# A one-core attention and FFN kernel: eight pooled PSUM banks, the token gate on VectorE, memory in column tiles, and a newly tuned instruction plan

## The chip, the cores and the metric

The kernel runs on one core of a Trainium2 chip. The metric is device microseconds of one execution. Most executions of one kernel agree within 0.3%. All runs told here are at a granted TensorE clock of 0.99 to 1.00. PE is TensorE (its matrix engine), DVE is VectorE, ACT is ScalarE, POOL is GpSimd, SP is the engine that issues most DMAs. PSUM is the memory that the matmuls of this kernel write, used as eight banks of 128x512 fp32; SBUF is the on-chip memory of its other tiles.

## The reference

Two branches read the same `x` (2048 tokens, 512 features) and are mixed by a gate per token. In short:

```python
g = sigmoid((x * gate_w).sum(-1, keepdims=True))        # one number per token
a = A(x)      # 32 heads of 16, 4 segments of 512 tokens, causal softmax inside a segment,
              # plus a linear memory carried from segment to segment:
#   a_mem = phi(q) @ M / (phi(q) @ z + 1e-6);   o = gh * a_mem + (1 - gh) * a_dot
#   M += phi(k).T @ v;  z += phi(k).sum()       # after each segment; then o @ wo
b = (relu(x @ W_gate) * (x @ W_up)) @ W_down            # 1792 wide
return g * a + (1 - g) * b
```

The kernel factors `1 - g` out, so that what the attention branch needs per token is the ratio `g / (1 - g)`.

## The kernel before

Nothing is scheduled by hand line by line. The program describes its work as tasks: an engine, an assumed duration, a priority (`key`, lower first), dependencies and a PSUM bank. A small list scheduler, the plan, runs over these tasks at build time with its assumed durations. The order in which it starts them becomes the order of instructions on each engine. On the chip each engine takes its instructions in that order: in the changed kernel's trace all 2214 matmuls fall on the plan's tasks one by one, in the order emitted. If an instruction is not ready, everything behind it on that engine waits (the chain near 57 us, below, shows it).

The parts that the change touches, with cuts marked:

```python
def run(self):                                   # the plan
    ...
    for t in sorted((t for t in ready if t.avail <= now), key=rank):
        if busy.get(t.eng, 0.0) > now: continue
        ...                                      # takes a PSUM bank if one is free
        if mode.get(t.eng) != t.mode:            # PE: full array, row tiles or column tiles
            t.dur += SWITCH + (126 if t.mode and mode.get(t.eng) else 0)
...
sp = psum.tile([P, 4, L], F32, name="sp")        # four banks: scores only
wb = [psum.tile([P, L], F32, name=f"wb{b}") for b in range(4)]   # four banks: all else
...
# assumed durations in ns, by engine
plan.add("DVE", 690, ...)   # a 128x512 eviction from PSUM
plan.add("DVE", 460, ...)   # KTe, KTo: masked copies of K transposed, SBUF to SBUF
plan.add("DVE", 830, ...)   # phi: two SBUF operations
plan.add("ACT", 1880, ...)  # exponential of 128x2048 scores
plan.add("POOL", 640 * len(diags), ...)          # causal mask of the exponentials, affine_select

def gate_tasks(seg):
    def pe():                                    # token gate: 16 matmuls with ONE column each
        for t in range(4):
            for ci in range(NC):
                nc.tensor.matmul(bank(sl)[:, t:t + 1], lhsT=xT[...], rhs=gw[:, ci:ci + 1], ...)
    a = plan.add("PE", 420, key, pe, ...)
    ...                                          # exp, then an fp32 matmul spreads the ratios
def memory(seg):                                 # M and z: 16 matmuls, 128 x 136, in two banks
    ...
    a = plan.add("PE", 1000, key, pe, ...)
```

A unit is four pairs of heads of one segment: 16 units in all. Each has five score fills (eight or four row-tiled matmuls into the four score banks), five exponentials on ACT, masks on POOL, and two groups of column-tiled value matmuls. Projections and FFN matmuls of 128x512 fill the rest of PE.

The softmax here doesn't subtract the row's maximum and nothing guards it: scores larger than these inputs give would overflow.

Of the kernel before, what the change touches and what calls it, by code (L numbers as in the profile page):

```python
# [12 lines left out]
P = 128  # L13
# [12 lines left out]
SWITCH = 100.0  # L26
RQ = 5
RE = 8
RH = 16


class Task:




    def __init__(self, eng, dur, key, emit, deps=(), lat=100, need=None, frees=(), after=None,
                 mode=None):
        self.eng, self.dur, self.key, self.emit, self.mode = eng, dur, key, emit, mode
        self.deps = [d for d in deps if d is not None]  # L40
        self.lat, self.need, self.frees, self.after = lat, need, tuple(frees), after
        self.avail = 0.0


class Slot:
    def __init__(self, kind):
        self.kind, self.banks, self.left = kind, (), 0


class Plan:  # L50



    def __init__(self, nbanks):
        self.tasks = []
        self.free = {i: 0.0 for i in range(nbanks)}

    def add(self, *a, **k):
        t = Task(*a, **k)
        self.tasks.append(t)  # L60
        return t

    def pick(self, slot, now):
        ok = [b for b in sorted(self.free) if self.free[b] is not None and self.free[b] <= now]
        if slot.kind == 2:
            for b in ok:
                if b % 2 == 0 and b + 1 in ok:
                    return (b, b + 1)
            return None
        for b in ok:  # L70
            if b ^ 1 not in ok:
                return (b,)
        return (ok[-1],) if ok else None

    def run(self):
        users = {}
        for t in self.tasks:
            t.wait = len(t.deps) + (t.after is not None)
            for d in t.deps:
                users.setdefault(id(d), []).append(t)  # L80
            if t.after is not None:
                users.setdefault(id(t.after), []).append(t)
            for s in t.frees:
                s.left += 1
        ready = [t for t in self.tasks if t.wait == 0]
        busy, mode = {}, {}
        now, order = 0.0, []
        left = len(self.tasks)
        while left:
            progressed = True  # L90
            while progressed:
                progressed = False
                def rank(t):
                    turn = t.mode and mode.get(t.eng) and t.mode != mode[t.eng]
                    return (bool(turn), t.key)
                for t in sorted((t for t in ready if t.avail <= now), key=rank):
                    if busy.get(t.eng, 0.0) > now:
                        continue
                    if t.need is not None and not t.need.banks:
                        got = self.pick(t.need, now)  # L100
                        if got is None:
                            continue
                        t.need.banks = got
                        for b in got:
                            self.free[b] = None
                    if mode.get(t.eng) != t.mode:
                        t.dur += SWITCH + (126 if t.mode and mode.get(t.eng) else 0)
                        mode[t.eng] = t.mode
                    t.start = now
                    busy[t.eng] = now + t.dur  # L110
                    t.done = now + t.dur + t.lat
                    order.append(t)
                    ready.remove(t)
                    left -= 1
                    for s in t.frees:
                        s.left -= 1
                        if s.left == 0:
                            for b in s.banks:
                                self.free[b] = t.done
                    for u in users.get(id(t), ()):  # L120
                        u.wait -= 1
                        u.avail = max(u.avail, t.start + t.dur if u.after is t else t.done)
                        if u.wait == 0:
                            ready.append(u)
                    progressed = True
            if not left:
                break
            times = [t.avail for t in ready if t.avail > now]
            times += [b for b in busy.values() if b > now]
            times += [f for f in self.free.values() if f is not None and f > now]  # L130
            assert times, "the plan is stuck"
            now = min(times)
        self.end = max(t.done for t in order)
        return order
# [3 lines left out]
def kernel(  # L138
# [21 lines left out]
    rpool = ctx.enter_context(tc.tile_pool(name="rpool", bufs=3))  # L160
    psum = ctx.enter_context(tc.tile_pool(name="psum", bufs=1, space=bass.MemoryType.PSUM))

    def sb(shape, dtype, name):
        return wpool.tile(shape, dtype, name=name)


    xT = [sb([P, NC, L], BF16, f"xT{i}") for i in range(3)]
    wq_sb = sb([P, NC, D], BF16, "wq_sb")
# [6 lines left out]
    gw = sb([P, NC], BF16, "gw")  # L175
    betab = sb([P, H], BF16, "betab")

    E = [sb([P, 4, L], BF16, f"E{i}") for i in range(RE)]
    x0 = E[RE - 1]
    clock = [3300.0]  # L180
    plan = Plan(4)

    def arrival(nbytes):
        clock[0] += nbytes / 340.0
        return plan.add("in%d" % len(plan.tasks), 0.0, 0.0, None, lat=clock[0])

    def load(eng, dst, src, nbytes):
        eng.dma_start(out=dst, in_=src)
        return arrival(nbytes)

    def load_cols(eng, t, ap, c0, c1):
        k = ap.shape[0] // P
        return load(eng, t[:, :, c0:c1], ap.rearrange("(c p) n -> p c n", p=P)[:, :, c0:c1],
                    k * P * (c1 - c0) * 2)

    def load_xT(seg):
        nc.sync.dma_start_transpose(out=xT[seg % 3][:], in_=x[seg * L:(seg + 1) * L, :])
        return arrival(L * D * 2 * 1.3)

    FP = [(0, 512), (512, 1024), (1024, 1408), (1408, F)]  # L200
    got_x, got_g, got_u = {}, {}, {}
    def load_halves(dst, src, k, nbytes):
        src = src.rearrange("(c p) n -> p c n", p=P)
        nc.sync.dma_start(out=dst[:, 0:k // 2], in_=src[:, 0:k // 2])  # L204
        nc.scalar.dma_start(out=dst[:, k // 2:k], in_=src[:, k // 2:k])
        return arrival(nbytes)

    got_x0 = load_halves(x0, x[0:L, :], 4, L * D * 2)
    got_q = [load_halves(wq_sb, A_wq, NC, D * D * 2)] * 2
    got_k = [load_cols(nc.sync, wk_sb, A_wk, 0, D)] * 2  # L210
    got_v = load_cols(nc.scalar, wv_sb, A_wv, 0, D)
    nc.scalar.dma_start(out=betab[:], in_=A_beta.partition_broadcast(P))
    with nc.allow_non_contiguous_dma(reason="1 KB"):
        nc.scalar.dma_start(out=gw[:], in_=gate_w.rearrange("(c p) -> p c", p=P))
    got_gw = arrival(0)

    def load_gu(i):
        got_g[i] = load_cols(nc.sync, wg_sb, B_W_gate, *FP[i])
        got_u[i] = load_cols(nc.sync, wu_sb, B_W_up, *FP[i])

    def load_wd(a, b):
        return load(nc.sync, wd_sb[:, a:b, :],
                    B_W_down.rearrange("(c p) n -> p c n", p=P)[:, a:b, :], (b - a) * P * D * 2)

    load_gu(0)
    load_gu(1)
    got_x[1] = [load_xT(1)]
    load_gu(2)
    load_gu(3)
    got_d = [load_wd(0, 7), load_wd(7, NF)]  # L230
    got_o = load_cols(nc.sync, wo_sb, A_wo, 0, D)
    got_x[2] = [load_xT(2)]


    junk = sb([P, L], BF16, "junk")
    nc.vector.memset(junk[:], 0.0)
# [7 lines left out]
    for j in range(4):  # L244
# [7 lines left out]
                            pattern=[[0, NC], [16, 8], [0, HW]], channel_multiplier=-1)  # L252

    fold = sb([P, 4, 32], F32, "fold")
    nc.gpsimd.memset(fold[:], 0.0)
    pbm = sb([P, 4], F32, "pbm")
    nc.vector.memset(pbm[:], 0.0)
    for b in range(4):
        nc.gpsimd.affine_select(out=fold[:], in_=fold[:], compare_op=ALU.not_equal, fill=1.0,
                                base=-32 * b, pattern=[[0, 4], [-1, 32]], channel_multiplier=1)  # L260
        nc.vector.memset(pbm[32 * b:32 * b + 32, b:b + 1], 1.0)
    rblk = sb([P, 4, 4], F32, "rblk")
# [5 lines left out]
    grc = [sb([P, NC, 2, 2, 16], F32, f"grc{i}") for i in range(2)]  # L268

# [11 lines left out]
    got_gates = plan.add("DVE", 900, 0.0, head_gates, [got_eb], 100)  # L281


    sp = psum.tile([P, 4, L], F32, name="sp")
    wb = [psum.tile([P, L], F32, name=f"wb{b}") for b in range(4)]
    QT = [sb([P, L], BF16, f"QT{i}") for i in range(RQ)]
    KTe = [sb([P, L], BF16, f"KTe{i}") for i in range(RQ)]
    KTo = [sb([P, L], BF16, f"KTo{i}") for i in range(RQ)]
    pqT = [sb([P, L], BF16, f"pqT{i}") for i in range(RQ)]
    pK = [sb([P, 4, D], BF16, f"pK{i}") for i in range(2)]  # L290
    Vp = [sb([P, 4, H, 18], BF16, f"Vp{i}") for i in range(2)]
    oT = [sb([P, NC, L], BF16, f"oT{i}") for i in range(2)]
    hT = [sb([P, L], BF16, f"hT{i}") for i in range(RH)]
    T = [sb([P, 2, L], F32, f"T{i}") for i in range(2)]
# [425 lines left out]
```

## Time and profile before

The time was 282.37 us (median of 3 runs, 282.19 to 282.45). The profiled execution has a span of 280.8 us. Two lines of its first page, span and busy time with the share of the span and the number of instructions:

```profile
span 280.8 us, 5327 instructions
...
PE 272.8 (97%) x2122; PEld 113.4 (40%) x2122; DVE 205.7 (73%) x427; ACT 196.6 (70%) x176; POOL 87.6 (31%) x144
```

Then the chain that ended last, followed back from the last instruction, by engine and by line of the kernel:

```profile
## 4 chain that ended last, share of the span: by engine, by line
PE 92%; ACT 3%; DMA 3%; DVE 1%; issue 0%; SPq 0%; ACTq 0%
```

PE is 92% of this chain. So PE sets the time and the others mostly keep up. But a busy PE is not a PE at its peak, so its time was taken apart from the starts of the matmuls in the trace. A 128x512 matmul streams in 216 ns, four row or column tiles together in the same time. Every change between full, row-tiled and column-tiled matmuls costs 93 to 98 ns more (median by kind of change, counted from start to start after subtracting the last group's streaming) and, averaged over whole stretches, about 117 ns. A stall is counted wherever the gap from start to start exceeds the streaming time, and 97 ns at a change, by more than 45 ns. The last row but one is what is left over, since changes are charged at 117 ns and stalls counted from 97. From the first transpose of x to the end of PE:

| part, us | before |
|---|---|
| streaming | 243.9 |
| 193 changes of tiling at 0.117 | 22.6 |
| one-column gate matmuls and fp32 folds, beyond streaming | 2.0 |
| memory matmuls, beyond streaming | 0.2 |
| stalls | 4.0 |
| left over | -1.3 |
| measured, 5.45 to 276.86 us | 271.4 |

Only about 6 us of this (gate, memory, stalls) is neither streaming nor changes of tiling, and of these two the change can save a little. The start is where 1.5 us of the stalls are. In the timeline of PE (start, duration, line, operation; a gap and what ended it in brackets) only half of the 16 Q matmuls run before PE waits for wk:

```profile
6.35 2.19 PE L327 MATMUL wb<-xT,wq_sb 128*128 128x512 bf16 x8
9.55 1.47 PE L327 MATMUL wb<-xT,wk_sb 128*128 128x512 bf16 x6 [1.01 <-DMA wk_sb<-in_A_wk_dram]
```

Three groups of instructions that come up again (count, then busy us and mean ns of one, then idle time before them): the masked K copy on DVE, the memory matmuls and the one-column gate matmuls.

```profile
L435 DVE TENSOR_SCALAR KTe<-kt,mcol_e 128x512 bf16<-128x512 bf16 x16 | 6.9, 436 | 0.1
...
L592 PE MATMUL wb<-Vp,pK 128*128 128x136 bf16 x48 | 3.5, 226 | 0.0
...
L360 PE MATMUL wb<-gw,xT 128*128 128x1 bf16 x64 | 2.2, 163 | 0.0
```

And DVE's busy time in stretches of 10 us (stretch, its length, busy us with the number of instructions, granted clock, DMA share, GB/s):

```profile
20.00:30.00 10.00, 7.89 (x20) 1.00 1.10 342
30.00:40.00 10.00, 8.85 (x20) 1.00 0.65 104
40.00:50.00 10.00, 8.28 (x16) 1.00 0.14 28
50.00:60.00 10.00, 8.10 (x19) 1.00 0.01 2
```

From 10 to 90 us DVE is busy 65.7 of 80 us, well above its 73% over the whole span.

### The profile page before, as it was taken

Reading aid. Unit: us, or ns where it says so; the run is one execution under the profiler, and the core shown is the slowest. Engines: PE = TensorE matmul, PEld = TensorE weight load, DVE = VectorE, ACT = ScalarE, POOL = GpSimd, SP = SyncE. Lnnn points to the kernel's source line nnn. Section 1 sums busy time; section 2 is a strip of 40 time slices with the busy share of each in tenths; the row PEclk is TensorE's granted clock in tenths of the full one; section 3 lists DMA queues with packets and bytes.
Section 4 is the critical chain, followed back from the end, with each engine's and each line's share of the span. In section 5 each row is a group of like instructions: output and inputs, shape, how many; then the busy total and the mean of one; then the engine's idle time right before and its main releaser. Section 6 shows DMA issues by size and latency. Waiting matters only on the chain.

```text
span 280.8 us, 5327 instructions
## 1 busy us (share of the span) xinstructions
PE 272.8 (97%) x2122; PEld 113.4 (40%) x2122; DVE 205.7 (73%) x427; ACT 196.6 (70%) x176; POOL 87.6 (31%) x144
## 2 busy tenths in 40 slices
PE   8899999999989999999999999999999999999994
PEld 3343444433434343343443344344434343444441
DVE  3588797798994768968997599957898966374221
ACT  3299797988886659888876779898897677723000
POOL 7014233334242332433343424443334243300000
PEclk9999999999999999999999999999999999999999
DMA  7999930013001010000001000000000010000011
GB/s 230 316 255 349 208 49 19 4 22 75 19 2 39 21 37 2 19 2 19 0 11 47 21 21 2 0 2 0 2 0 2 19 39 21 0 2 0 0 37 39
DMA packets 24488, 13.71 MB, mean 49 GB/s; under 512 B 13968, under 2 KB 24464, under 8 KB 24464
## 3 DMA queue, kind: packets, MB, share of 16 engines
q1 hardware_dynamic: 22720, 12.32, 16.5%
q10 hardware_dynamic: 1744, 1.06, 1.3%
q8 instruction: 16, 0.26, 0.4%
q14 instruction: 8, 0.07, 0.1%
HBM read 8.14 MB, written 2.10 MB: 36 GB/s over the span
## 4 chain that ended last, share of the span: by engine, by line
PE 92%; ACT 3%; DMA 3%; DVE 1%; issue 0%; SPq 0%; ACTq 0%
PE wb L327 73%; PE sp L478 9%; PE wb L518 7%; DMA wk_sb<-in_A_wk_dram 3%; ACT E L499 2%; PE wb L574 2%; PE wb L592 1%; ACT rg L628 1%; PE wb L360 1%; SPq L204 0%; DVE osb L658 0%; DVE T L547 0%; PE wb L380 0%; ACT e L416 0%; ACTq L628 0%
## 5 line engine op out<-in xcount | busy, mean ns | idle before, releaser
L499 ACT ACTIVATE E<-sp 128x2048 bf16<-128x2048 f32 x80 | 150.4, 1880 | 37.0 <-PE sp L478 33.0
L505 POOL TENSOR_SCALAR_AFFINE_SELECT E<-E 128x512 bf16<-128x512 bf16 x128 | 82.5, 660 | 156.0 <-ACT E L499 156.0
L327 PE MATMUL wb<-xT,wg_sb 128*128 128x512 bf16 x224 | 59.7, 380 | 0.0
L327 PE MATMUL wb<-xT,wu_sb 128*128 128x512 bf16 x224 | 59.3, 380 | 0.4 <-ACT rg L628 0.4
L327 PE MATMUL wb<-wd_sb,hT 128*128 128x512 bf16 x224 | 54.1, 380 | 0.0
L635 DVE TENSOR_TENSOR hT<-wb,rg 128x512 bf16<-128x512 f32 x56 | 38.1, 682 | 17.7 <-PE wb L327 9.7
L547 DVE STREAM_TRANSPOSE T<-wb 128x512 f32<-128x512 f32 x56 | 36.7, 693 | 14.9 <-PE wb L518 9.0
L628 ACT ACTIVATE rg<-wb 128x512 bf16<-128x512 f32 x56 | 33.0, 602 | 13.8 <-PE wb L327 13.8
L327 PEld LDWEIGHTS <-hT 128*128 128x128 bf16 x224 | 20.4, 98 | 26.1 <-issue 4.2
L327 PEld LDWEIGHTS <-wu_sb 128*128 128x128 bf16 x224 | 20.3, 98 | 26.2 <-issue 5.0
L327 PEld LDWEIGHTS <-wg_sb 128*128 128x128 bf16 x224 | 19.8, 98 | 25.3 <-issue 5.5
L658 DVE TENSOR_SCALAR osb<-wb,ngcol 128x512 bf16<-128x512 f32 x16 | 11.9, 741 | 17.7 <-PE wb L327 17.6
L558 DVE TENSOR_TENSOR o<-T,cf 128x512 bf16<-128x512 f32 x28 | 20.1, 718 | 1.0
L518 PE MATMUL wb<-E,Vp 128*17 128x256 bf16 (+3 forms) x512 | 20.4, 300 | 0.0
L478 PE MATMUL sp<-QT,KTo 32*128 32x512 bf16 (+3 forms) x256 | 17.1, 299 | 0.8 <-ACT E L499 0.8
L478 PE MATMUL sp<-QT,KTe 32*128 32x512 bf16 (+3 forms) x256 | 17.3, 302 | 0.3 <-ACT E L499 0.3
L327 PE MATMUL wb<-xT,wk_sb 128*128 128x512 bf16 x64 | 16.5, 380 | 1.0 <-DMA wk_sb<-in_A_wk_dram 1.0
L327 PE MATMUL wb<-wo_sb,oT 128*128 128x512 bf16 x64 | 17.1, 380 | 0.0
L327 PE MATMUL wb<-wv_sb,xT 128*128 128x512 bf16 x64 | 16.8, 380 | 0.2 <-DVE T L547 0.2
L327 PE MATMUL wb<-xT,wq_sb 128*128 128x512 bf16 x64 | 16.7, 380 | 0.1
L408 DVE CAST QT<-wb 128x512 bf16<-128x512 f32 x16 | 11.0, 688 | 6.8 <-PE wb L327 4.4
L518 PEld LDWEIGHTS <-Vp 128*17 128x17 bf16 x512 | 10.7, 91 | 13.0 <-issue 4.2
(70 smaller groups left out, 192.9 us busy)
## 6 DMA issues: line engine op xcount, KB each, us to landing
out_dram<-osb SPq DMA_DIRECT2D x16, 128.0 KB, 1.7
wd_sb<-in_B_W_down_dram SPq DMA_DIRECT2D x2, 896.0 KB, 8.4
wg_sb<-in_B_W_gate_dram SPq DMA_DIRECT2D x2, 512.0 KB, 9.6
wu_sb<-in_B_W_up_dram SPq DMA_DIRECT2D x2, 512.0 KB, 10.0
wg_sb<-in_B_W_gate_dram SPq DMA_DIRECT2D x2, 384.0 KB, 5.2
wu_sb<-in_B_W_up_dram SPq DMA_DIRECT2D x2, 384.0 KB, 5.2
wk_sb<-in_A_wk_dram SPq DMA_DIRECT2D x1, 512.0 KB, 7.7
wv_sb<-in_A_wv_dram ACTq DMA_DIRECT2D x1, 512.0 KB, 9.1
```

The costliest lines, as they stand in the source:

```text
L327: nc.tensor.matmul(bank(sl), lhsT=lhsT, rhs=rhs, start=(start and q == 0), stop=(stop and q == n - 1))
L408: prj["q", seg, c] = plan.add("DVE", 690, key - RQK, lambda: nc.vector.tensor_copy(QT[i][:], bank(sl)), [a], DVL, frees=[sl])
L478: nc.tensor.matmul(sp[:, j, off:off + n], lhsT=kt[32 * j:32 * j + 32, kb * P:(kb + 1) * P], rhs=QT[i][32 * j:32 * j + 32, kb * P:kb * P + ...
L499: b = plan.add("ACT", 1880, key, lambda Ef=Ef: nc.scalar.activation(Ef[:], sp[:], ACT.Exp, scale=SCALE), [a] + eread.get(n - RE, []), ACL)
L505: nc.gpsimd.affine_select(out=m, in_=m, compare_op=ALU.is_ge, fill=0.0, base=0, pattern=[[0, 4], [1, P]], channel_multiplier=-1)
L518: nc.tensor.matmul(wb[sl.banks[0]][32 * j:32 * j + HW, kb * P:kb * P + w], lhsT=Vp[i][:, kb, 8 * c + 2 * j + r, 0:HW], rhs=E[(5 * u + f) % ...
L547: done.append(plan.add("DVE", 700, key - RL, lambda r=r, sl=sl: nc.vector.transpose(T[m][:, r], bank(sl)), [a, att.get(("part", m, u - 1)) ...
L558: nc.vector.tensor_tensor(dst[0].rearrange("p (q r e) -> p r q e", r=2, e=DH), t[:, :, :, 0:DH], cf[:, :, :, None].to_broadcast([P, 2, 16, ...
L574: a = plan.add("PE", 216, key + r, lambda r=r, sl=sl: nc.tensor.matmul(bank(sl), lhsT=mbd[i][:, c, r].rearrange("p j e -> p (j e)"), rhs=p ...
L628: nc.scalar.activation(rg[0][:], bank(sl), ACT.Relu)
L635: nc.vector.tensor_tensor(hT[(NF * seg + fv) % RH][:], bank(sl), rg[0][:], ALU.mult)),
L658: nc.vector.tensor_scalar(osb[0][:], bank(sl), ngcol[:, tt:tt + 1], None, ALU.mult)
```

## The change

Its intent is fivefold. All eight PSUM banks become one pool, and score banks may be lent to other work when no fill is near. The token gate leaves PE: DVE multiplies and sums, and for segments 1 to 3 the ratios are spread over the partitions by DMA through DRAM. The memory matmuls run as four column tiles, chained behind the value matmuls of a unit. Buffers become rings that the plan knows, and load times come from a table of landing times. Last, the plan gets new durations, a rule that column tiles may be followed by row tiles at once, and a table that shifts the keys of some 140 single tasks. The diff, cut to its core:

```diff
-SWITCH = 100.0
-RE = 8
+SWITCH = 119.0
+LOOK = 1500.0
+RE = 7
+SHIFT = {33: 140000, 77: 9000, 81: 150000, ...}      # about 140 entries
 ...
-                    return (bool(turn), t.key)
+            return (t.mode == "col" and mode.get(t.eng) == "row", t.key, t.n)
 ...
-    sp = psum.tile([P, 4, L], F32, name="sp")
-    wb = [psum.tile([P, L], F32, name=f"wb{b}") for b in range(4)]
+    ps = psum.tile([P, 8 * L], F32, name="ps")
+    def work():
+        return plan.one("ps", range(7, -1, -1))
 ...                                                     # the token gate
-        a = plan.add("PE", 420, key, pe, got_x[seg] + [got_gw], PEL, need=sl)
+        for t in range(4):
+            zs.append(plan.add("DVE", 640, key, lambda t=t: nc.vector.scalar_tensor_tensor(
+                junk[:], xn[seg % 2][:, t, :], 1.0, gwb[:], ALU.mult, ALU.mult,
+                accum_out=zc[:, 4 * seg + t:4 * seg + t + 1]), [got_n[seg], got_gw], 60))
 ...                                                     # durations, some of many
-        prj["q", seg, c] = plan.add("DVE", 690, key - RQK, lambda: nc.vector.tensor_copy(
+        prj["q", seg, c] = plan.add("DVE", 600, key - RQK, lambda: nc.vector.tensor_copy(
-            plan.add("DVE", 460, key, lambda: nc.vector.tensor_scalar(     # KTe
+            plan.add("DVE", 268, key, lambda: nc.vector.tensor_scalar(
-        b = plan.add("DVE", 830, key + 500, ph, [b, d], DVL)               # phi
+        b = plan.add("DVE", 747, key + 500, lambda: phi(...), [b, d], DVL, need=[pk], ...)
-            masks.append(plan.add("POOL", 640 * len(diags), key, mk, [b], POL))
+            masks.append(plan.add("POOL", 593 * len(pieces), key, mk, exps, POL))
 ...                                                     # the memory
-        a = plan.add("PE", 1000, key, pe, ...)
+                    for j in range(4):
+                        nc.tensor.matmul(bank(sl)[32 * j:32 * j + 32, 34 * g:34 * g + 34], ...,
+                            tile_position=(0, 32 * j))
+        a = plan.add("PE", 530, key - PVP, pe, ..., mode="col")
+        plan.link([att["pv", u], a])
 ...
+    for n, d in SHIFT.items():
+        plan.tasks[n].key += d
     order = plan.run()
```

## The prediction

> **What bounds the kernel now.** TensorE, nearly alone. The chain of waits gives PE 92% of the 280.8 us span, and the windows view shows it busy 20.00 of 20 us from 140 us to 260 us. VectorE is 73%, ScalarE 70% busy; the last score exponential ends at 243 us and 33 us of pure FFN matmuls follow, so attention is not late. Granted clock 1.00.
>
> I summed matmul start to start in the trace, from the first x transpose (5.4 us) to PE's end (276.9 us), 271.4 us:
> - streaming at 216 ns per 512 columns (a quarter of that for four row or column tiles): 243.9 us
> - 193 changes between full, row-tiled and column-tiled matmuls at about 117 ns each: 22.6 us
> - the token gate on PE: 16 one-column matmuls (0.38 us) and an fp32 fold, four times: 2.0 us beyond streaming
> - start: 8 of 16 Q matmuls, then 1.17 us idle until wk lands at 9.55 us, and slow first matmuls: 1.7 us
> - real stalls (behind relu, an exponential, a transpose): about 2.2 us
>
> After PE: eviction 0.75 us and the output DMA, 4.0 us in all. The Trainium skill (TensorEngine Tiling (Array Packing), Key Properties) says a change of tiling mode drains TensorE; the trace agrees with 117 ns a change. All 80 score fills stay, so most of those 22.6 us stay.
>
> **What the change does, on the chain.**
> - Gate matmuls leave PE; only segment 0 keeps a fold: -1.7 us. In their place VectorE gets 16 multiply-and-sum operations of about 0.65 us (estimate from its 0.53 to 0.7 us 128x512 operations), +10 us busy, 73% to about 78%: off the chain. The DRAM round trip (two landings of about 2 us, as the output's 1.7 us) is off the chain too.
> - Memory in column tiles: 2.99 us in three pieces becomes about 1.6 us (16 groups of four at about 33 ns, estimated from 50 ns per four 128-column tiles), linked behind the last column-tiled value matmuls, so no mode change is added: -1.3 us.
> - Score fills may now directly follow value matmuls, which the old plan avoided (one case in the trace, costing one change instead of two). I expect half of 16: -1 us.
> - Eight banks and measured landing times: all Q matmuls can run before wk lands: -1.2 us at the start. Mid-kernel, lending saves perhaps half of the stalls, -0.8 us (could be +1).
> - Last tile in halves: the last eviction halves: -0.4 us.
>
> Sum about -6.5 us. Rings, and an E ring of 7 instead of 8: nothing.
>
> **Predicted:** 275.6 us (ratio 0.976), 8 in 10 between 273.2 and 278.4. Faster by over 2%: 0.66; within 2%: 0.32; slower by over 2%: 0.02.
>
> **What the profile would show.** No one-column matmuls and no fp32 folds but segment 0's; memory matmuls about 0.5 us each; 16 Q matmuls back to back before K, no idle near 8 us; PE's last matmul near 270.5 us; VectorE near 215 us busy, ScalarE near 196; mode changes down from 193 to about 180; a score fill starting right behind value matmuls in about half of the units; last eviction near 0.37 us.
>
> **What would make it wrong.** The new order is tuned hard (over a hundred shifted keys) against modelled durations shorter than the traced ones (605 against 682 ns for the relu product). If VectorE falls behind, eight banks only hide it and PE stalls 2 to 4 us: then within 2%. If the plan merges nearly all value and score runs and removes every stall, 273. Lent score banks could delay a fill behind an eviction; with 33 us of slack at the end that costs little.

## The result, and the profile after

The changed kernel took 281.55 us (median of 4 runs, 280.95 to 282.01), against 282.35 us before. The ratio is 0.9966, with a 95% interval of 0.9951 to 0.9982. Ratios here and below are the mean time of one kernel's fast runs over that of the other kernel's fast runs of the same rounds, so they are not quite the ratio of the medians quoted. The prediction was 275.6 us with a range of 273.2 to 278.4: the result lies outside.

The first page and the chain after:

```profile
span 279.2 us, 5541 instructions
...
PE 270.2 (97%) x2214; PEld 112.8 (40%) x2214; DVE 214.0 (77%) x456; ACT 196.3 (70%) x176; POOL 88.6 (32%) x139
...
## 4 chain that ended last, share of the span: by engine, by line
PE 72%; DVE 18%; DMA 5%; ACT 2%; issue 1%; SPq 1%; DVEq 0%; ACTq 0%
```

PE's share of the chain fell from 92% to 72% and DVE's rose from 1% to 18%. The same account of PE, with the best kernel of the experiments beside it:

| part, us | before | after | best (tuned_robust) |
|---|---|---|---|
| streaming | 243.9 | 241.7 | 241.7 |
| changes of tiling | 22.6 (193) | 20.9 (179) | 20.9 (179) |
| one-column gate and folds | 2.0 | 0.2 | 0.1 |
| memory, beyond streaming | 0.2 | 0.8 | 0.9 |
| stalls | 4.0 | 8.1 | 4.2 |
| left over | -1.3 | -1.1 | -1.0 |
| measured | 271.4 | 270.6 | 266.8 |

Every saving that was predicted for the gate, the memory and the changes of tiling arrived. The groups show it: 192 small memory matmuls in column tiles for 48 large ones, no one-column matmuls, and the gate sums on DVE.

```profile
L411 DVE SCALAR_TENSOR_TENSOR junk<-xn,gwb 128x512 bf16<-128x512 bf16 x16 | 12.3, 767 | 0.5 <-DMA gwb<-in_gate_w_dram 0.4
...
L524 DVE TENSOR_SCALAR KTe<-ktr,mcol_e 128x512 bf16<-128x512 bf16 x16 | 7.4, 465 | 0.0
...
L683 PE MATMUL ps<-Vp,pK 128*32 128x34 bf16 x192 | 2.0, 183 | 0.0
```

The stalls ate it up: 8.1 us instead of 4.0. They are not spread evenly. Between 10 and 90 us they were 1.6 us before (0.7 us of it up to 80 us) and are 5.7 us after. The DVE stretches after, for the same times as above:

```profile
20.00:30.00 10.00, 9.20 (x25) 1.00 1.09 347
30.00:40.00 10.00, 9.32 (x20) 1.00 0.84 159
40.00:50.00 10.00, 9.76 (x24) 1.00 0.32 79
50.00:60.00 10.00, 9.76 (x23) 1.00 0.17 55
```

All 16 gate sums run between 13.9 and 90.3 us, and DVE is now busy 75.1 of the 80 us from 10 to 90. The chain in order of time (start, us, what) shows what PE stood behind near 57 us: one long row of DVE work, from the KT copy and a gate sum (L411) to two transposes of value results.

```profile
56.67 0.72 DVE KTo L527
57.38 0.61 DVE junk L411 x2
57.99 0.60 DVE hT L724
58.59 0.09 DVE rp L421
58.70 0.18 DVE ngcol L422
58.88 0.67 DVE pkT L492
59.60 0.04 issue
59.64 0.42 DVE pkT L493
60.06 1.22 DVE T L639 x2
```

The plan's own start times make this sharper. Each task was matched with its instructions in the trace, engine by engine. PE ran behind the changed kernel's plan by 0.3 us at 11 us, 1.5 at 31, 2.3 at 51, 3.5 at 64 and 4.9 at 77 us, and by 4.7 to 5.6 us from there to the end. The plan ends at 273.4 us; the chip ended at 279.2. The kernel before runs behind its plan by up to 1.6 us early and by 0.2 us at the end; its assumed durations are on the whole too long (its plan gives VectorE 220.7 us, and the trace has it busy for 205.7).

The start did gain something: twelve Q matmuls run before wk lands instead of eight, and the stalls of the first 10 us went from 1.5 to 0.8 us.

```profile
6.97 2.75 PE L458 MATMUL ps<-xT,wq_sb 128*128 128x512 bf16 x12 [0.23 <-ACT xT L482]
9.79 1.04 PE L458 MATMUL ps<-xT,wk_sb 128*128 128x512 bf16 x4
```

Lending, the first part of the change's name, hardly happens. In the order that the plan emits, 242 times a bank is taken for other work than scores. Only 12 of these are of the four score banks, all after 239 us, when the last fills are over. (The profile does not show bank numbers; this is counted in the emitted program.)

### The profile page after: what moved, and what is told of

It is laid out like the page before. It is cut to its first block, busy times and chain, and to the rows that moved or that the text cites. A ratio compares the mean times of both kernels' runs of the same rounds, so it can differ in the third digit from the quotient of the medians.

```text
span 279.2 us, 5541 instructions
## 1 busy us (share of the span) xinstructions
PE 270.2 (97%) x2214; PEld 112.8 (40%) x2214; DVE 214.0 (77%) x456; ACT 196.3 (70%) x176; POOL 88.6 (32%) x139
## 4 chain that ended last, share of the span: by engine, by line
PE 72%; DVE 18%; DMA 5%; ACT 2%; issue 1%; SPq 1%; DVEq 0%; ACTq 0%
PE ps L458 58%; PE ps L567 7%; PE ps L609 6%; DMA gwb<-in_gate_w_dram 3%; DVE hT L724 2%; DVE ktr L521 2%; DVE junk L411 2%; DVE T L639 2%; PE ps L665 2%; DVE pkT L493 1%; DMA xn<-in_A_x_dram 1%; ACT ex L497 1%; DVE KTe L524 1%; DVE pkT L492 1%; DVE KTo L527 1%
## 5 line engine op out<-in xcount | busy, mean ns | idle before, releaser
L587 ACT ACTIVATE E<-ps 128x2048 bf16<-128x2048 f32 x80 | 150.4, 1880 | 30.8 <-PE ps L567 25.0
L458 PE MATMUL ps<-xT,wg_sb 128*128 128x512 bf16 x224 | 58.0, 380 | 0.4 <-DVE hT L724 0.2
L458 PE MATMUL ps<-xT,wu_sb 128*128 128x512 bf16 x224 | 56.9, 379 | 0.7 <-DVE Vp L550 0.5
L458 PE MATMUL ps<-wd_sb,hT 128*128 128x512 bf16 (+1 forms) x238 | 54.8, 367 | 0.0
L724 DVE TENSOR_TENSOR hT<-ps,rgr 128x512 bf16<-128x512 f32 x56 | 37.9, 681 | 16.0 <-PE ps L458 10.6
L718 ACT ACTIVATE rgr<-ps 128x512 bf16<-128x512 f32 x56 | 32.6, 601 | 18.2 <-PE ps L458 18.1
L639 DVE STREAM_TRANSPOSE T<-ps 128x512 f32<-128x512 f32 x56 | 37.4, 694 | 9.7 <-PE ps L609 9.1
L609 PE MATMUL ps<-E,Vp 128*17 128x256 bf16 (+3 forms) x512 | 21.0, 300 | 0.9 <-DVE hT L724 0.9
L650 DVE TENSOR_TENSOR och<-T,cfr 128x512 bf16<-128x512 f32 x28 | 19.3, 696 | 0.3
L458 PE MATMUL ps<-xT,wk_sb 128*128 128x512 bf16 x64 | 17.7, 380 | 0.9 <-DVE T L639 0.8
```

What stands on the lines that cost most here:

```text
L458: nc.tensor.matmul(bank(sl)[:, 0:width], lhsT=lhsT, rhs=rhs, start=(start and q == 0), stop=(stop and q == n - 1))
L587: nc.scalar.activation(Ef[:, e0 * L:e1 * L], ps[:, e0 * L:e1 * L], ACT.Exp, scale=SCALE),
L609: nc.tensor.matmul(bank(sl)[32 * j:32 * j + HW, kb * P:kb * P + w], lhsT=Vp[i][:, kb, 8 * c + 2 * j + r, 0:HW], rhs=E[(NFILL * u + f) % RE ...
L639: done.append(plan.add("DVE", 633, key - RL, lambda r=r, sl=sl: nc.vector.transpose(T[ts.i][:, r], bank(sl)), [a] + done, DVL if r else 0, ...
L650: nc.vector.tensor_tensor(och[ds.i].rearrange("p (q r e) -> p r q e", r=2, e=DH), t()[:, :, :, 0:DH], cfr[cs.i][:, :, :, None].to_broadcas ...
L718: r = plan.add("ACT", 478, key - RL, lambda sl=gsl, rs=rs: nc.scalar.activation(rgr[rs.i][:], bank(sl), ACT.Relu), [g], ACL, frees=[gsl])
```

## The experiments

Theories. A: the gate sums overload VectorE in the first 90 us. B: the instruction order was made from durations that the chip does not keep, and PE pays wherever the order is tight. C: lent banks and early work crowd PSUM. Later D: it is GpSimd's masks, running at the same time, that make VectorE slower than the plan believes. Kernels named as wrong give a wrong result on purpose. Every run was timed in three rounds against the kernel before on the same chip (281.9 to 283.9 us there).

| run | median us | ratio to before | PE stalls us |
|---|---|---|---|
| after | 281.55 | 0.9966 | 8.1 |
| nogate (wrong) | 278.37 | 0.9850 | 5.5 |
| lategate | 280.14 | 0.9913 | 7.4 |
| noshift | 282.72 | 1.0001 | 8.5 |
| meas_noshift | 279.48 | 0.9897 | 5.4 |
| late_m | 278.45 | 0.9850 | 5.0 |
| pegate_m | 281.50 | 0.9976 | 6.0 |
| nogate_m (wrong) | 278.94 | 0.9877 | 5.4 |
| tuned_m | 276.84 | 0.9804 | 4.3 |
| tuned_late | 278.39 | 0.9853 | 6.1 |
| tuned_robust | 276.07 | 0.9788 | 4.2 |
| tuned_nogate (wrong) | 275.79 | 0.9770 | 3.4 |
| before_short | 286.77 | 1.0158 | 8.9 |
| nomask (wrong) | 276.47 | 0.9800 | 4.3 |
| before_nomask (wrong) | 282.43 | 1.0001 | 4.3 |

The traces of late_m, pegate_m and nogate_m lack 36 matmul records each (2178 for 2214, and 2242 for 2278); 216 ns for each missing one was taken off their stalls.

### Take the gate sums off VectorE, order unchanged (nogate)

```diff
-  nc.vector.scalar_tensor_tensor(junk[:], xn[...][:, t, :], 1.0, gwb[:], ALU.mult, ALU.mult,
-      accum_out=zc[:, 4 * seg + t:4 * seg + t + 1])
+  nc.vector.tensor_tensor(zc[:, 4 * seg + t:4 * seg + t + 1], xn[...][:, t, 0:1], gwb[:, 0:1], ALU.mult)
```

> Same instruction order as the changed kernel, but each of the 16 token-gate sums on VectorE (about 0.76 us with its accumulator read, all between 13.9 and 90.3 us) becomes a one-column product (wrong result on purpose). Theory A (the gate sums overfill VectorE in the first 90 us, and PE pays for the overrun there): PE stalls between 10 and 90 us fall from 5.7 us to under 2.5 us, and the time falls from 281.6 to about 277.5 us. Theory B (the instruction order was tuned on durations that are too short, so PE stalls wherever the order is tight, gate or no gate): stalls stay above 4 us, time above 280 us. Theory C (lent score banks and early work crowd PSUM): same as B here.

It took 278.37 us, 3.2 us less. Stalls from 10 to 90 us fell to 3.0 us, not below 2.5, and about 3 us of the miss were still there. So VectorE's time in this stretch matters, which speaks for A, but something else is left.

### Issue the gate sums of segments 2 and 3 later (lategate)

```diff
     order = plan.run()
+    LATE = {2: (90e3, 92e3, 94e3, 96e3, ...), 3: (140e3, 142e3, 144e3, 146e3, ...)}
+    for seg, at in LATE.items():
+        for t, s in zip(gated[seg], at):
+            t.start = s
+    order.sort(key=lambda t: t.start)
```

> Same kernel, correct result: only the eight gate sums of segments 2 and 3 and what follows them are issued later (at 90 to 105 us and 140 to 155 us of the plan, where VectorE has room), all else in the same order. Theory A: about 5 us of VectorE work leaves the crowded stretch of 47 to 90 us; PE stalls there fall by 1.5 to 3 us and the time falls to about 279.5 us. Theories B and C: no change beyond 0.5 us (281.5 us).

280.14 us, 1.4 us less. PE stalls between 50 and 90 us fell from 3.2 to 0.8 us as A expects, but new ones appeared where the sums went: 1.4 us between 150 and 160 us, where there had been none. In a fixed order every insertion disturbs what was tight there. This made B more likely.

### An order without the shifts (noshift), and with traced durations (meas_noshift)

```diff
-    for n, d in SHIFT.items():
-        plan.tasks[n].key += d
```

> The table of shifted keys is emptied, so the list scheduler makes its own order from the same durations. The plan itself says this costs 2.1 us. If the tuned order is worth on the chip what the plan says, 283.7 us. If the tuning fitted only the plan's own durations (B), no worse than the changed kernel, 281 to 282 us or less.

```diff
-  "ACT", 66 + (e1 - e0) * L / 1.2          # exponential, 1773
+  "ACT", 1824
-  "POOL", 593 * len(pieces)
+  "POOL", 664 * len(pieces)
-  "DVE", 747 (phi)   268, 268 (KTe, KTo)   640 (gate sum)   605 (relu product)   600 (evictions)
+  "DVE", 850         370, 340              750              630                  615
-  "ACT", 478 (exp of phi)   478 (relu)
+  "ACT", 520                542
-  "DVE", 930 (scaling of the value results)   631 (sum of the two attention parts)
+  "DVE", 660                                  450        # these two had been too long
                                            # and so on for all tasks; no shifts
```

> Empty table of shifts as in the run before, and every task's duration set to the mean that the chip took in the changed kernel's trace (exponential 1824 instead of 1773 ns, mask 664 instead of 593, phi 850 instead of 747, gate sum 750 instead of 640, and so on). Theory B: the plan, now honest, orders around VectorE; it beats the run without shifts by 2 us or more and the changed kernel by 1 us or more (280.5 us or less). Theory A: VectorE has the same work, order alone cannot help it; within 1 us of the run without shifts, and VectorE still above 92% busy from 20 to 80 us.

Without shifts the kernel took 282.72 us. That lies between its two expectations: the shifts were worth about 1.1 us, where the plan said 2.1. With the durations of the trace and still no shifts it took 279.48 us: 3.2 us faster than the same work in the other order, and 2 us faster than the tuned kernel. The chains of the two, noshift first:

```profile
PE 69%; DVE 19%; ACT 6%; issue 4%; POOL 0%; DVEq 0%; ACTq 0%
...
PE 83%; ACT 5%; DVE 5%; DMA 3%; issue 1%; POOL 0%; SPq 0%; ACTq 0%
```

Not all of the plan's durations had been too short: on VectorE the edit lengthens most tasks, by 14.5 us in all, and shortens two kinds, by 9.7 us. What each correction is worth was not tried. VectorE was as busy as ever (74.8 of 80 us from 10 to 90). So theory A alone fails, and B holds. In this order PE is at most about 0.6 us behind its plan. No bank of the scores is lent in it either, so lending is worth nothing here, and theory C is out as far as it rests on lent banks.

### Both together (late_m, nogate_m), and the gate back on PE (pegate_m)

```diff
 # late_m, on top of meas_noshift
-        key = KA(4 * seg - 3)
+        key = KA(4 * seg - 2)
 # nogate_m, on top of meas_noshift: gate sums as in nogate, planned at 60 ns
 # pegate_m, on top of meas_noshift: the old 16 one-column matmuls, one clip on DVE
```

> The run with traced durations and no shifts (279.5 us), with one more edit: the key of the gate work of each segment is one unit later, so VectorE does the gate sums after more urgent work. Correct result. If both causes hold (sums that crowd VectorE early, and an order made from durations that are too short), they add: 277.5 us or less, stalls of PE in all below 4 us. If the honest durations alone already healed what the sums did, no change: 279 to 280 us. The plan says 275.8 instead of 278.2 us.

> Both suspected costs taken away at once (wrong result on purpose): traced durations, no shifts, and gate sums of one column planned at 60 ns. If the two causes make up the whole miss, 275.5 to 277 us, close to the 275.6 us that was predicted; if a third cause is left, above 277.5 us.

> Traced durations and no shifts as in the 279.5 us run, but the token gate is back on TensorE (16 one-column matmuls a segment, 0.38 us each segment), its ratios still spread by DMA. VectorE loses 13.6 us of work, PE gains about 1.6 us. If VectorE's load is what costs, this beats the 279.5 us run by 1 to 2.5 us (277 to 278.5 us) although PE has more to do. If not, it is 1.5 us slower (281 us).

late_m took 278.45 us, a gain of 1.0 us instead of 2, between its two expectations. nogate_m took 278.94 us, no better: once the durations are honest, taking the gate sums away altogether gains 0.5 us, where it gained 3.2 us in the order made from short ones. By its expectation a third cause was left. Stalls of 5.4 us remained; that order, like every one without shifts, was not searched any further. pegate_m took 281.50 us, near the second of its expectations (281), but not for the reason given there: its PE ended only 0.8 us after that of meas_noshift, with 1.6 us of gate matmuls and a single 1.7 us stall behind ScalarE at 179.5 us, and in the profiled run its last output landed 4.0 us after issue instead of the usual 1.7. Its order is new as a whole, so whether the gate belongs on PE stays open.

### A new search of the shifts on honest durations (tuned_m, tuned_late, tuned_robust)

The plan alone, with traced durations, was searched for 13 minutes by random changes of keys. tuned_robust judges each order by the mean of five plans, in four of which all durations are off by a random 6%. tuned_late and tuned_robust also have the later gate key of late_m, so tuned_robust differs from tuned_late in its shifts alone.

```diff
-SHIFT = {33: 140000, ...}             # found on the short durations
+SHIFT = {...}                         # found on the traced durations; some 840 entries
```

> The changed kernel with traced durations in its plan and with a new table of shifts, found by a random search on that plan (13 minutes); gate sums stay early on VectorE. Correct result. The plan ends at 272.8 us, where without shifts it ended at 278.2 and the chip's span was 277.2. Theory B (the order's worth depends on the durations it was made from): the tuned order now holds on the chip, span 272.5 to 275 us, time 274.5 to 277 us, at least 2.5 us faster than the 279.5 us run and near the 275.6 us predicted. If any hard-tuned order breaks on the chip whatever its durations: span 277 us or more, no gain over the untuned order. Theory A alone (VectorE's load): little gain, since VectorE has the same work before 90 us.

> The same search, with the gate sums one unit later as in the 278.45 us run; the plan ends at 273.4 us. Theory B: time 275 to 277.5 us. If the late gate sums give the order more room for errors than the plan sees, it beats the tuned run with early sums although its plan is 0.6 us longer.

> As the run before, but each order of the search was judged by the mean of five plans, four of them with every duration off by a random 6%, so that it should break less on the chip; the plan ends at 273.7 us. If fragility of a tuned order is what is left, this beats both other tuned runs by 0.5 us or more; if not, it is 0.3 us slower, as its plan says.

tuned_m took 276.84 us and tuned_robust 276.07 us, 2.1% faster than the kernel before (interval 0.977 to 0.981). Both results are correct. This is the whole change, with no work added or taken away, only another order. The interval reaches to both sides of 2%. tuned_late, whose plan was 0.3 us shorter than tuned_robust's, took 278.39 us, over its expected 275 to 277.5: it fell 3.0 us behind its plan, and tuned_robust 0.9. One search of each kind does not prove that the noise was what helped.

Two limits belong here. The new tables have some 840 entries and the old one 141, and a search as long on the short durations was not run: how much of the 3.4 us between meas_noshift and tuned_robust is the durations, and how much the longer search, is not shown. And a tuned order still loses on the chip: tuned_m's plan gained 5.4 us over meas_noshift's (278.2 to 272.8), the chip 2.6.

tuned_robust's first page and VectorE's stretches:

```profile
span 275.4 us, 5546 instructions
...
PE 269.1 (98%) x2214; PEld 113.5 (41%) x2214; DVE 214.2 (78%) x456; ACT 197.0 (72%) x176; POOL 90.1 (33%) x139
...
PE 82%; DVE 10%; ACT 3%; issue 2%; DMA 2%; DVEq 0%; ACTq 0%
```

```profile
20.00:30.00 10.00, 9.79 (x27) 1.00 1.07 345
30.00:40.00 10.00, 9.24 (x19) 1.00 0.99 175
40.00:50.00 10.00, 9.90 (x24) 1.00 0.48 117
50.00:60.00 10.00, 9.18 (x22) 1.00 0.11 16
```

VectorE has the same 214 us of work and is just as full early on (75.8 of 80 us), yet PE's stalls are halved. A full VectorE need not stop PE, if what PE needs next is what VectorE does next.

### The two cross checks (tuned_nogate, before_short)

```diff
 # tuned_nogate: tuned_robust with the gate sums cut as in nogate, order unchanged
 # before_short: the kernel before, six kinds of durations
-  "DVE", 690    "ACT", 600    "ACT", 1880    "DVE", 830    "DVE", 460    "POOL", 640 *
+  "DVE", 600    "ACT", 478    "ACT", 1773    "DVE", 747    "DVE", 268    "POOL", 593 *
```

> The 276.1 us kernel, same order, with its 16 gate sums cut to one column (wrong result on purpose), as was done to the changed kernel, which gained 3.2 us from it. If VectorE's load by itself costs PE (A), again 2 us or more: 274 us or less. If the sums hurt only where the order had been made from too short durations (B), under 1 us: 275.1 to 276.2 us.

> The kernel before, with the changed kernel's short durations in its plan (evictions 600 instead of 690 ns, relu 478 instead of 600, exponential 1773 instead of 1880, masks 593 instead of 640, KT copies 268 instead of 460, phi 747 instead of 830) and nothing else: same work, new order; its plan ends 0.5 us earlier. Theory B: its stalls of 4.0 us grow, it becomes 1 to 4 us slower (283.5 to 286 us). If short durations do no harm where VectorE is only 82% full from 10 to 90 us (A: load and short durations must meet), within 1 us of 282.3 us.

tuned_nogate gained 0.3 us where nogate had gained 3.2. And the kernel before, given nothing but the changed kernel's short durations (the value transposes too, 633 for 700 ns, which the expectation does not list), became 4.4 us slower, 286.77 us, a little more than the 1 to 4 us expected. Its plan claimed a gain of 0.5 us. Its stalls rose from 4.0 to 8.9 us, and its chain turned from 1% to 15% VectorE although VectorE's busy time was 204.6 us, 1.1 us less than before:

```profile
## 4 chain that ended last, share of the span: by engine, by line
PE 74%; DVE 15%; ACT 4%; DMA 3%; issue 2%; SPq 0%; DVEq 0%; ACTq 0%
```

Of the 4.9 us more stalls, 0.5 us were wk, which landed 0.7 us later in that trace.

### Why the durations of SBUF operations are too short (nomask, before_nomask)

The timeline of the changed kernel around 56 us shows the same operation with two durations. The copy that ends before the mask on POOL is well under way takes 0.34 us, and the two that meet it take 0.72 us:

```profile
55.77 0.34 DVE L527 TENSOR_SCALAR KTo<-ktr,mcol_o 128x512 bf16<-128x512 bf16 x1
55.92 1.32 POOL L596 TENSOR_SCALAR_AFFINE_SELECT E<-E 128x512 bf16<-128x512 bf16 x2 [0.86 <-ACT E L587]
56.03 0.72 DVE L524 TENSOR_SCALAR KTe<-ktr,mcol_e 128x512 bf16<-128x512 bf16 x1
...
56.67 0.72 DVE L527 TENSOR_SCALAR KTo<-ktr,mcol_o 128x512 bf16<-128x512 bf16 x1
```

Over the whole trace the KTe copy takes 345 ns (median of 7) with no mask beside it and 646 ns (median of 9) with one, and the phi product of K 426 and 732 ns. Evictions from PSUM do not care: the relu product has a mean of 683 ns alone and 679 with a mask. The Trainium skill (SBUF — State Buffer, the section on its two separate sides) says that VectorE and GpSimd share one pair of SBUF ports, "an exclusive lock, not a bandwidth split", which whoever starts first holds for the whole instruction, and names the VectorE operations concerned: those in a two-port mode, or with two SBUF inputs if the GpSimd operation reads SBUF, as the masks do. The trace agrees in what is slowed, what is not, and who holds. Of the 17 KTe and KTo copies that overlap a mask, the 5 that started before it took 340 to 348 ns, as alone, and 4 of these 5 masks took 680 to 803 ns instead of their median of 635. Of the 12 that started during a mask, 11 took 405 to 724 ns and ended 145 to 149 ns after that mask; the twelfth met only its last 85 ns and took 346. A general slowdown would not leave their ends at a fixed distance from the mask's.

```diff
-   m = Ef.rearrange("p (j q) -> p j q", j=4)[:, :, o:o + P]
+   m = Ef.rearrange("p (j q) -> p j q", j=4)[:, :, o:o + 4]      # and pattern [1, P] -> [1, 4]
```

> The changed kernel in its own order, with the GpSimd masks cut from 128 to 4 columns (wrong result on purpose). In the trace a VectorE copy of KT takes 345 ns alone and 646 ns (medians) when a mask runs at the same time, where the plan has 268; the phi products 425 and 733. Theory D (this overlap is what makes the plan's durations too short): KT copies and phi products fall to their lone durations, VectorE's busy time falls by 5 us or more, PE stalls fall from 8.1 to under 5.5 us, and the time to about 278.5 us. Rival (the overlap is only a coincidence of crowded stretches): the copies keep their long durations and the time stays above 280.5 us.

> The same cut of the masks in the kernel before, whose plan has 460 ns for the KT copies, 830 for phi, and VectorE 82% full from 10 to 90 us. Theory D with slack: VectorE gains as much, but PE was hardly waiting for it, so the time falls by less than 0.8 us (281.5 to 282.4 us). If shorter masks speed any kernel (earlier masks, earlier value matmuls), it gains 1.5 us or more as well.

With the masks cut, the changed kernel in its own order took 276.47 us, 5.1 us less, more than expected. The copy is back at its lone duration, and VectorE's busy time fell from 214.0 to 201.7 us (the masks of the changed kernel first, then four lines of nomask):

```profile
L596 POOL TENSOR_SCALAR_AFFINE_SELECT E<-E 128x512 bf16<-128x512 bf16 x128 | 85.0, 679 | 149.2 <-ACT E L587 149.2
...
PE 267.7 (97%) x2214; PEld 112.2 (41%) x2214; DVE 201.7 (73%) x456; ACT 196.1 (71%) x176; POOL 34.6 (13%) x139
...
PE 84%; DVE 5%; DMA 4%; ACT 4%; issue 1%; SPq 0%; ACTq 0%
...
L596 POOL TENSOR_SCALAR_AFFINE_SELECT E<-E 128x16 bf16<-128x16 bf16 x128 | 30.9, 255 | 197.8 <-ACT E L587 197.8
...
L524 DVE TENSOR_SCALAR KTe<-ktr,mcol_e 128x512 bf16<-128x512 bf16 x16 | 5.4, 343 | 0.0
```

The same cut in the kernel before changed nothing: 282.43 us, although VectorE lost 9.8 us of busy time there too (205.7 to 195.9). So shorter masks were no gain by themselves there, and in the changed kernel no wait of PE is put down to GpSimd. The next table has the time that a task holds VectorE (from its start to the next start, or to its own end if there is a gap), against what the changed plan assumes:

| task, ns | plan | after | nomask |
|---|---|---|---|
| KTe copy | 268 | 383 | 263 |
| KTo copy | 268 | 332 | 256 |
| phi, both operations | 747 | 857 | 698 |
| gate sum with accumulator read | 640 | 726 | 642 |
| value transposes (from PSUM) | 633 | 636 | 637 |
| relu product (from PSUM) | 605 | 630 | 637 |
| scaling of the value results | 930 | 651 | 646 |
| sum of the two attention parts | 631 | 418 | 398 |

For the copies and the gate sum the plan's durations are within 12 ns those of a VectorE without GpSimd beside it; for phi they lie between the two. The last two rows were too long, by about 10 us over the kernel, so the whole of VectorE's plan, 210.6 us, is near the 214.0 that it was busy. What matters is where the errors lie: the tasks of the plan's first 75 us held VectorE 69.4 us where 66.3 were planned (64.0 with the masks cut), just where it had no room, and this is the stretch in which PE fell behind. With the masks cut, PE is at most about 1.4 us behind the plan, and 0.35 us at the end, where with them it was 4.9.

## Why the prediction was wrong, point by point

- **"What bounds the kernel now": right.** PE, 92% of the chain.
- **Gate off PE, -1.7 us: right.** Its overhead went from 2.0 to 0.2 us.
- **Memory in column tiles, -1.3 us: right.** Streaming and overhead went from 3.0 to 1.5 us.
- **Score fills behind value matmuls, -1 us: right, and more.** 13 of 16 instead of half, 14 changes fewer, -1.6 us.
- **The start, -1.2 us: half right, for the wrong reason.** The stalls of the first 10 us fell by 0.65 us. Twelve Q matmuls ran early, not 16, and no score bank was lent to them.
- **Last tile in halves, -0.4 us: right in kind.** The last eviction took 0.48 us, not 0.37, and the time from PE's end to the end of the span fell from 4.0 to 3.1 us.
- **The step that failed: "Mid-kernel, lending saves perhaps half of the stalls, -0.8 us (could be +1)".** Lending happened 12 times in 242, after 239 us. All stalls together went from 4.0 to 8.1 us. Without those of the first 10 us they went from 2.5 to 7.3, +4.8 us where the sum had -0.8. This one term is worth 5.6 us, nearly all of the 6 us between 275.6 and 281.55. What stood in its place was the wait that the sum had left out: PE behind VectorE, in an order made from durations that the chip did not keep.
- **Beside it: VectorE "73% to about 78%: off the chain".** 77% was measured, and the conclusion was wrong. The mean hides 66 of 80 us in the stretch where all 16 sums land. The skill's page Perfetto Trace Analysis (Optimization Strategy) warns that the most-contended engine can change over time; here it did (from 40 to 60 us VectorE was busy 19.5 us of 20 and PE 18.9), and the question to ask was how busy VectorE is from 10 to 90 us.
- **The prediction named the risk** ("modelled durations shorter than the traced ones ... PE stalls 2 to 4 us: then within 2%"), with the numbers of the relu product, and gave it one chance in three. It took the wrong example: the relu product comes from PSUM and held VectorE 630 ns against 605, nearly what the plan says. The trace's duration of an instruction overlaps with the next (above, the KTo copy of 55.77 ends at 56.11, after KTe's start at 56.03), so 682 ns was not the number to hold against 605. The wrong ones were the SBUF copies, 383 against 268. The trace of the kernel before already showed a KTe mean of 436 ns, and the copy held VectorE 360 ns there; set beside the diff's 268, this would have told.

What is shown: with the same work, an order made from durations that the chip keeps takes 279.48 us without any search and 276.07 us, nearly the predicted gain, with one; the short durations alone slow the old kernel by 4.4 us; and taking the masks' time away, with the short-duration order kept, recovers 5.1 us. What is only argued: that it is the ports that are locked; the times show that the copy waits for the mask's end, and not on what. What stays open: why pegate_m was slow, how much of tuned_robust's gain is the longer search, and how much of its last 4.2 us of stalls another search would win.

## What to carry to other kernels

If a build-time plan orders the instructions, its durations are part of the kernel: calibrate each against the time that the task holds its engine in the trace of the kernel at work, with its neighbours running, and tune only then. Judge an added load by the stretch where it lands, not by the engine's share of the whole span. When VectorE copies inside SBUF show two durations, look at what GpSimd does at that moment.

## What the Trainium skill lacked or had wrong

- SBUF — State Buffer describes the lock between VectorE and GpSimd but not what it costs a kernel: here 128x512 bf16 copies went from 345 to 646 ns (medians), those that started during a mask ended 145 to 149 ns after it, VectorE was busy 12.3 us of 214 less when the masks went from 85 to 31 us on GpSimd, and in a tight order that was 5.1 us of the time.
- TensorEngine Tiling (Array Packing) says that a change of tiling mode drains TensorE and gives no number: 93 to 98 ns from start to start beyond the streaming in all directions seen. A direct change from column to row tiles costs 98 ns, one change and not two.
- No page that was read says that a hand-made instruction order must be planned with contended durations; the runs give 4.4 and 5.1 us for it.
